# A fused attention, soft mixture and feed-forward kernel: w_in kept by halves, four more weight slots, and the first unit of the feed-forward stage cut in two

## The chip, the cores and the metric

The kernel runs on one NeuronCore of one Trainium2 chip. Its engines are TensorE (PE, with its weight loads shown as PEld), VectorE (DVE), ScalarE (ACT), GpSimd (POOL) and SyncE (SP, which here only issues DMAs). The metric is the device time of one execution in microseconds (us). The time before is a median of 460.08 us over 3 runs, from 459.59 to 461.58 us. The execution that the profiler took lasted 463.19 us, of which the recorded span is 461.4 us.

## The reference

Three layers, one after the other. The inputs are float32, but for w_in and w_out, which come as float64; the output is float32.

```python
# 1. causal attention, 4 batches x 8 heads, 576 tokens, 64 wide
scores = q @ k.T / 8
bias   = -(cumsum(max(s, 0))[:, None] - cumsum(max(s, 0))[None, :])
attn   = softmax(where(causal, -1e9, scores + min(bias, 0)))
x      = attn @ v                        # gathered to [2304, 512]
# 2. soft mixture: 32 slots, 8 experts with 4 slots each
logits = x @ phi
slot_input = softmax(logits, tokens).T @ x          # [32, 512]
slot_out[e] = max(slot_input[e] @ w1[e], 0) @ w2[e] # w1 512x1024, w2 1024x512
x = softmax(logits, slots) @ slot_out
# 3. feed-forward
h = x @ w_in                             # 512 -> 2048
g = where(h >= 1, h, where(h <= -1, 0, (h + 1)**2 / 4))
out = g @ w_out                          # 2048 -> 512
```

The kernel never forms the second x. Since x = c @ slot_out with c of 32 columns, h = c @ (slot_out @ w_in), and the product M = slot_out @ w_in is only 32 x 2048. M is kept as a stack of 96 rows (`mst`: its rounded part twice, its rest once), against 96 rows of c (`cstack`), so that one matmul in the fast fp32r type gives h to float32's precision.

## The kernel before

**Attention.** 16 pairs of heads run one after the other. Each has four groups of score matmuls (line 291), row maxima on DVE (line 305), exponentials on ACT (line 350), transposes and products with v on PE. A table of numbers (`PLAN`, 12 units of plan time to a pair) says when each step's instructions are written, and `GATE` does so for the gating of one batch, which falls into the pairs 5, 9 and 13 and the one after each.

**Conversion of w_in.** It arrives as float64 words, 2048 columns by 512, in four quarters `fb` of 512 columns (a quarter is 2 MB raw and 1 MB as float32). During attention a generator (`convert_wi`) brings it chunk by chunk: a 256 KB DMA to `st`, one POOL operation (line 626), then two DVE operations (lines 627 and 629); each call of the generator issues one of the two. The pairs 1 to 13 call it, up to five times each. All four quarters stay in `wif`, 32 KB per partition. `finish_wi` later runs four DVE operations on each of 16 tiles.

**Weights of the experts.** w1 and w2 of 8 experts are 64 tiles of 512 KB, loaded by SP (line 140) into slots. 22 slots exist from the start (16 of kind "post", 6 of kind "pre"), filled during attention; 13 are cut out of attention's right-hand memory when that is free, 3 more after it; from there on a load waits for a slot that PE has done with. SP issues in program order and waits in place, so a load that waits holds all that is behind it.

**Experts.** For each expert `layer1` (line 736, 16 matmuls), a transpose, `layer2` (line 752, 32 matmuls). The last one gives `soT`, the transposed slot outputs.

**Feed-forward.** 96 units (j, c), j one of 6 blocks of 384 tokens, c one of 16 blocks of 128 hidden columns. A unit is: `h_part` (one matmul at line 879, relu and square on ACT at 881 and 882), `g_part` (max on DVE at 889, rounding to gh on ACT at 891), `l_part` (the rest gl on DVE at 897), `o_part` (nine matmuls at 907 to 909). The output matmuls of a unit are written two units after its `h_part`. The first 32 units alternate between j = 0 and 1, so that c advances every second unit, and through the first 30 of them w_out is converted (`convert_wo`: ACT at 154 and 786, DVE at 156, 158 and 788), one tile of 512 columns per two units. Its raw tiles come into "pre" slots.

M is computed ahead of the loop, in parts, by `m_part`: 16 matmuls of 128 columns for the first 128 columns of each quarter, all four quarters at once in four groups of 32 rows, then 16 of 384 columns. `split_m` writes the first quarter's stack on ACT and DVE, `stack_m` moves the other three quarters' rows into place by nine DMAs. The order is

```python
m_part(0, M_A, range(4))
split_m(0, M_A)
...
h_part(*seq[0])
h_part(*seq[1])
m_part(M_A, 512, range(1, 4))
g_part(*seq[0])
g_part(*seq[1])
```

Of the kernel before, what the change touches and what calls it, by code (L numbers as in the profile page):

```python
# [8 lines left out]
F32 = mybir.dt.float32  # L9
# [22 lines left out]
N_HOME = 16  # L32
N_LEFT = 6
N_RIGHT = 6
N_TMP = (7, 3)
# [15 lines left out]
WI_0 = (0,)  # L51
WARM_T = (9, 4, 2, 3, 4)
PRE_FROM, PRE_STEP = (5, 2.4)
# [3 lines left out]
BLK = 384  # L57

# [13 lines left out]
def attention_softmoe_ffn_kernel(  # L72
# [31 lines left out]
    wif = wip.tile([128, 4, 4, 512], F32, name="wif")  # L104

    w_src = {"w1": w1, "w2": w2, "wo": w_out.bitcast(I32)}
    w_tiles, w_wo, wo_used = {}, {}, []
# [58 lines left out]
    with att:  # L166
# [436 lines left out]
        for n in range(N_HOME + N_LEFT):  # L603
            at(3 * int(PRE_FROM + PRE_STEP * n) + 0.76, lambda: next(pre, None))

        def convert_wi():

            n_all = 2048 * 4 // CHUNK
            sts = {}

            def get(n):
                if n < n_all:
                    fb, k = divmod(n, 2048 // CHUNK)
                    sts[n] = stage.tile([128, 2 * CHUNK], I32, tag="st", name="st")
                    nc.sync.dma_start(out=sts[n], in_=w_in.bitcast(I32)[fb, :, 2 * CHUNK * k:2 * CHUNK * (k + 1)])

# [3 lines left out]
            for n in range(n_all):  # L620
                fb, k = divmod(n, 2048 // CHUNK)
                st = sts.pop(n)
                d = wif[:, fb].rearrange("p c f -> p (c f)")[:, CHUNK * k:CHUNK * (k + 1)]
# [3 lines left out]
                V.tensor_scalar(lo, lo, 1, 0x70000000, op0=ALU.logical_shift_right, op1=ALU.bitwise_and)  # L627
                yield
                V.tensor_tensor(out=d.bitcast(I32), in0=d.bitcast(I32), in1=lo, op=ALU.bitwise_or)
                get(n + 2)  # L630
                yield

        def finish_wi():

            for n in range(16):
# [11 lines left out]
        for pi in range(NP):  # L647
# [15 lines left out]
            for k in range(5) if pi else WI_0:  # L663
                step(f"W{k}", next, cw, None)
# [178 lines left out]
    M_A = 128  # L843
    mp = [ps_e.tile([128, 512], F32, tag="e", name="mp") for _ in range(2)]

    def m_part(a, b, cs):
        for c in cs:
            for fb in range(4):
                T.matmul(out=mp[a > 0][32 * fb:32 * fb + 32, a:b], lhsT=soT[:, c], rhs=wif[:, fb, c, a:b],
                         start=(c == 0), stop=(c == 3))  # L850

    m_hi = fin[0].tile([128, 512], F32R, tag="m_hi", name="m_hi", bufs=1)
    m_lo = fin[0].tile([128, 512], F32R, tag="m_lo", name="m_lo", bufs=1)
    ps_w = []

    def split_m(a, b):
# [158 lines left out]
```

## Time and profile before

| | |
|---|---|
| median of 3 runs | 460.08 us |
| profiled execution | 463.19 us (span 461.4 us) |
| PE busy | 443.8 us, 96% of the span |
| ACT busy | 339.0 us, 73% |
| DVE busy | 326.7 us, 71% |
| POOL busy | 45.3 us, 10% |
| DMA | 71.02 MB, mean 154 GB/s over the span |

The shares are averages over three stages with different limits. Attention lasts to about 193 us, the experts from there to 237 us, the feed-forward stage to the end. A busy PE in this table includes matmuls that stand in its pipeline and wait, so that 96% does not say that nothing else sets the time; the chain of waits and the stretches do.

### The profile page before, as it was taken

What the parts mean: (1) busy time and instruction counts of PE and PEld (TensorE: products, weight loads), DVE (VectorE), ACT (ScalarE), POOL (GpSimd) and SP (SyncE); (2) the same over time, 40 slices, a digit from 0 to 9 for tenths busy, and PEclk for the clock granted to TensorE, in tenths of its full rate; (3) what the DMA queues carried; (4) which work ended last, traced back from release to release, by engine and by line L of the source; (5) the groups of instructions that cost most, each with busy time, mean ns of one, the idle gap of its engine ahead of it and who ended that gap; (6) DMA issues with size and microseconds to landing.
All of it is one profiled execution on the core that took longest, in us unless ns stands there. A gap on an engine that the chain in (4) does not pass through costs nothing.

```text
span 461.4 us, 11656 instructions
## 1 busy us (share of the span) xinstructions
PE 443.8 (96%) x4306; PEld 336.8 (73%) x4306; DVE 326.7 (71%) x966; ACT 339.0 (73%) x914; POOL 45.3 (10%) x168
## 2 busy tenths in 40 slices
PE   7999999999999998898889999999999999999996
PEld 2676766776777676566546888888888888888885
DVE  6687899899988863699838888866555555455543
ACT  6998998998999894122248999977677767777673
POOL 2222212422222111000000000000000000000000
PEclk9799999999999998799999999999999999999999
DMA  3888879977897258699985900003001001001001
GB/s 86 228 219 217 255 218 294 265 225 192 221 279 237 67 170 287 216 390 407 409 294 196 362 2 1 0 2 136 1 0 68 1 1 70 1 0 56 14 1 68
DMA packets 28554, 71.02 MB, mean 154 GB/s; under 512 B 4018, under 2 KB 5490, under 8 KB 28498
## 3 DMA queue, kind: packets, MB, share of 16 engines
q1 hardware_dynamic: 28342, 70.14, 47.7%
q8 instruction: 34, 0.56, 0.5%
q14 instruction: 22, 0.18, 0.2%
q10 hardware_dynamic: 156, 0.14, 0.1%
HBM read 64.83 MB, written 4.83 MB: 151 GB/s over the span
## 4 chain that ended last, share of the span: by engine, by line
PE 83%; DVE 6%; DMA 5%; ACT 4%; issue 2%; POOL 0%; ACTq 0%; POOLq 0%; DVEq 0%; SPq 0%
PE o L909 14%; PE o L907 14%; PE o L908 14%; PE s L291 9%; PE s L399 7%; PE s L360 5%; DMA wt<-in_w_dram 4%; PE hp L879 4%; PE s L434 3%; PE p L736 2%; PE s L299 2%; PE s L391 2%; PE p L752 2%; ACT P L350 1%; DVE s L305 1%
## 5 line engine op out<-in xcount | busy, mean ns | idle before, releaser
L907 PE MATMUL o<-wt,gh 128*128 128x512 f32 x288 | 112.6, 391 | 0.6 <-ACT gh L891 0.6
L909 PE MATMUL o<-wt,gl 128*128 128x512 f32 x288 | 112.3, 390 | 0.2 <-DVE gl L897 0.2
L908 PE MATMUL o<-wt,gh 128*128 128x512 f32 x288 | 112.1, 389 | 0.0
L350 ACT ACTIVATE P<-s,nm 128x256 f32<-128x256 f32 (+4 forms) x160 | 85.0, 551 | 9.1 <-DVE nm L305 6.8
L897 DVE TENSOR_TENSOR gl<-g,gh 128x384 fp32r<-128x384 f32 x96 | 53.5, 557 | 42.1 <-ACT gh L891 42.0
L305 DVE CUSTOM_DVE_ANT_0 s<-s,tri 128x256 f32<-128x256 f32 (+4 forms) x160 | 74.0, 506 | 12.6 <-PE s L291 6.2
L891 ACT CAST gh<-g 128x384 fp32r<-128x384 f32 x96 | 49.3, 513 | 45.1 <-DVE g L889 42.6
L889 DVE SCALAR_TENSOR_TENSOR g<-w,hp 128x384 f32<-128x384 f32 x96 | 53.1, 553 | 37.2 <-ACT w L882 37.2
L907 PEld LDWEIGHTS o<-wt,gh 128*128 128x128 f32 x288 | 54.3, 188 | 12.8 <-ACT gh L891 1.1
L909 PEld LDWEIGHTS o<-wt,gl 128*128 128x128 f32 x288 | 54.0, 188 | 12.5 <-DVE gl L897 1.3
L908 PEld LDWEIGHTS o<-wt,gh 128*128 128x128 f32 x288 | 54.4, 189 | 7.5
L291 PE MATMUL s<-x 64*128 64x512 f32 (+3 forms) x256 | 57.1, 471 | 0.0
L881 ACT ACTIVATE w<-hp,half 128x384 f32<-128x384 f32 x96 | 55.4, 577 | 0.8 <-PE hp L879 0.8
L882 ACT ACTIVATE w<-w 128x384 f32<-128x384 f32 x96 | 50.4, 525 | 3.0
L383 ACT COPY pts<-s 128x512 f32<-128x512 f32 (+3 forms) x128 | 47.8, 463 | 1.5 <-PE s L360 0.5
L360 PEld LDWEIGHTS s<-ident,P 64*128 64x128 f32 x800 | 38.6, 142 | 10.9 <-ACT P L350 4.8
L360 PE MATMUL s<-ident,P 64*128 64x64 f32 x800 | 44.2, 229 | 2.3 <-ACT P L350 2.2
L399 PE MATMUL s<-pts,v 128*64 128x512 f32 (+3 forms) x256 | 38.9, 446 | 0.0
L350 ACT ACTIVATION_READ_ACCUMULATOR P<-s,nm 128x1 f32 x160 | 36.8, 230 | 0.0
L879 PE MATMUL hp<-cstack,mst 96*128 96x384 f32 x96 | 32.6, 343 | 0.3 <-DVE mst L859 0.3
L291 PEld LDWEIGHTS s<-x 64*128 64x128 f32 x256 | 29.3, 196 | 4.2 <-DMA x<-in_qkT_dram 1.5
L399 PEld LDWEIGHTS s<-pts,v 128*64 128x64 f32 x256 | 18.5, 141 | 17.5 <-issue 15.3
(149 smaller groups left out, 567.2 us busy)
## 6 DMA issues: line engine op xcount, KB each, us to landing
wt<-in_w_dram SPq DMA_DIRECT2D x64, 512.0 KB
x<-in_qkT_dram SPq DMA_DIRECT2D x32, 288.0 KB
st<-in_w_in_dram SPq DMA_DIRECT2D x32, 256.0 KB
wt<-in_w_out_dram SPq DMA_DIRECT2D x16, 512.0 KB
out_dram<-ob SPq DMA_DIRECT2D x17, 256.0 KB
v<-in_v_main_dram SPq DMA_DIRECT2D x16, 256.0 KB
ext<-exts SPq DMA_DIRECT2D x60, 3.4 KB
v<-in_v_tail_dram SPq DMA_DIRECT2D x16, 32.0 KB
```

The source lines that it names most:

```text
L291: T.matmul(out=o[h][:, off:off + n], lhsT=y[r, 0, c:c + 128], rhs=y[r, 1, 0:n], start=(k == 0), stop=(k == 1))
L305: V.tensor_tensor_reduce(out=sc, in0=sc, in1=mask[:, mask.shape[1] - n:], scale=-1.0 / SCALE, scalar=init, op0=ALU.add, op1=ALU.min, accum ...
L350: A.activation(out=out_, in_=in_, func=AF.Exp, bias=nm, scale=-1.0, accum_out=sm[:, k:k + 1])
L360: T.transpose(out=o[f][:, c:c + 64], in_=P[r], identity=ident[r, r])
L399: T.matmul(out=o[r, 128 * j:512], lhsT=vt[:, j, r], rhs=pts_t[pi][:, h, 512 * j:384 * j + 512], start=(j == 0), stop=(j == 3))
L879: T.matmul(out=hp, lhsT=mst[0:96, 128 * c:128 * c + 128], rhs=cstack[0:96, BLK * j:BLK * j + BLK], start=True, stop=True)
L881: A.activation(out=w, in_=hp, func=AF.Relu, bias=half, scale=0.5)
L889: V.scalar_tensor_tensor(out=g, in0=w, scalar=1.0, in1=hp, op0=ALU.min, op1=ALU.max)
L897: V.tensor_tensor(out=gl, in0=g, in1=gh.bitcast(F32), op=ALU.subtract)
L907: T.matmul(out=o_t[j][t], lhsT=gh[:, r], rhs=wh[c], start=(c == 0), stop=False)
L908: T.matmul(out=o_t[j][t], lhsT=gh[:, r], rhs=wl[c], start=False, stop=False)
L909: T.matmul(out=o_t[j][t], lhsT=gl[:, r], rhs=wh[c], start=False, stop=(c == 15))
```

## The change

The quarters of w_in get three fates. Quarters 0 and 1 stay in `wif` as before (`WI_KEEP`). Quarter 2 is converted in attention too, wholly, with three DVE operations per chunk, and each chunk is stored to a DRAM tile (`w_in_f`), to be read back after the experts' weights (`WI_AWAY`). Quarter 3 is loaded raw after the experts' weights and converted inside the feed-forward loop, in four pieces at the units 5, 8, 11 and 14 (`WI_LATE`, `LATE_AT`). `wif` so needs 16 KB per partition less, and four more weight slots take that place (`N_LEFT` 6 to 10). The generator is called in the pairs of `W_PAIRS` alone, five times each, and twice in pair 0; 26 weight loads are spread over attention and not 22.

The first 128 columns of M are computed three times into 96 rows, so that the stack is one cast over 96 rows and one subtraction. The first unit's activation is done in a part of 128 and one of 256 tokens. M's quarter 2 and 3 are computed inside the loop, in the units 10 and 18 (`M_AT`), by 16 matmuls each, and stacked by twelve DMAs per quarter.

```diff
-N_LEFT = 6
+N_LEFT = 10
+WI_KEEP = 2
+WI_AWAY = (2,)
+WI_LATE = (3,)
+W_PAIRS = (1, 2, 3, 4, 6, 7, 8, 10, 11, 12, 14)
...
-WI_0 = (0,)
+WI_0 = (0, 3)
-PRE_FROM, PRE_STEP = (5, 2.4)
+PRE_AT = [3 * int(5 + 2.4 * _n) + 0.76 for _n in range(22)] + [171.76, 177.76, 183.76, 186.76]
+M_AT = {10: 2, 18: 3}
+LATE_AT = 5
...
                 G.tensor_scalar(d, hi.bitcast(F32), 2.0 ** -112, 1.0, op0=ALU.mult, op1=ALU.mult)
-                V.tensor_scalar(lo, lo, 1, 0x70000000, op0=ALU.logical_shift_right, op1=ALU.bitwise_and)
+                if away:
+                    V.tensor_scalar(lo, lo, 29, None, op0=ALU.logical_shift_right)
+                    yield
+                    V.scalar_tensor_tensor(out=di, in0=di, scalar=3, in1=lo, op0=ALU.logical_shift_left, op1=ALU.bitwise_or)
+                    yield
+                    V.scalar_tensor_tensor(out=di, in0=hi, scalar=-0x80000000, in1=di, op0=ALU.bitwise_and, op1=ALU.bitwise_or)
+                else:
...
+                get(n + 2)
+                put()
+                if away:
+                    spill.append((fb, k, d))
                 yield
...
-            for n in range(16):
+            for n in range(4 * WI_KEEP):
...
+    def load_wi():
+
+        for fb in WI_LATE:
+            for c in range(4):
+                raw, slot = slot_tile(I32)
+                nc.sync.dma_start(out=raw, in_=w_in.bitcast(I32)[fb, :, 1024 * c:1024 * c + 1024])
...
+                late.append((convert(raw, out_, out_), slot))
+        for fb in WI_AWAY:
+            for n in range(2):
+                t = slot_tile()[0]
+                nc.sync.dma_start(out=t, in_=w_in_f[fb][:, 1024 * n:1024 * n + 1024])
...
+    def h_part(j, c, fb=None):
+        hm = ps_h.tile([128, 512], F32, tag="h", name="hp")
+        hp = hm[:, 0:BLK]
         T.matmul(out=hp, lhsT=mst[0:96, 128 * c:128 * c + 128], rhs=cstack[0:96, BLK * j:BLK * j + BLK], start=True, stop=True)
+        if fb is not None:
+            m_part(hm[:, BLK:512], back(fb))
...
+    def first_m():
+
+        m = ps_o.tile([96, 128], F32, tag="o1", name="m0")
+        for c in range(4):
+            for r in range(3):
+                T.matmul(out=m[32 * r:32 * r + 32, :], lhsT=soT[:, c], rhs=wif[:, 0, c, 0:128], start=(c == 0), stop=(c == 3))
+        A.copy(out=mst[0:96, 0:128], in_=m)
+        V.tensor_tensor(out=mst[64:96, 0:128], in0=m[64:96], in1=mst[64:96, 0:128].bitcast(F32), op=ALU.subtract)
...
+    load_wi()
     one_c = gens[WO_EARLY]
     next(one_c)
-    m_part(0, M_A, range(4))
-    split_m(0, M_A)
     next(one_c)
+    first_m()
+    m_part(mp[0], kept(0))
+    first_unit()
+    h_part(*seq[1])
+    for fb in range(1, WI_KEEP):
+        m_part(mp[fb], kept(fb))
     next(one_c)
-    m_part(M_A, 512, range(1))
-    h_part(*seq[0])
-    h_part(*seq[1])
-    m_part(M_A, 512, range(1, 4))
-    g_part(*seq[0])
     g_part(*seq[1])
...
+    for g in range(1, 4):
+        split_m(mp[0], g)
+    for fb in range(1, WI_KEEP):
+        stack_m(fb, mp[fb])
...
+        for n, k in late_at.get(i, []):
+            for _ in range(k):
+                next(late[n][0])
```

SP's queue from the end of attention to the feed-forward stage, before (wt is an expert's or w_out's tile, gate a wait for the last expert weight, mst M's stack):

```order
L140 DMA wt<-in_w_dram 128x1024 x38
L140 DMA wt<-in_w_out_dram 128x1024
L140 DMA wt<-in_w_dram 128x1024 x4
L140 DMA wt<-in_w_out_dram 128x1024
L133 DMA gate<-wt 1x1
L140 DMA wt<-in_w_out_dram 128x1024 x6
L867 DMA mst<-m_hi 32x512 x2
L867 DMA mst<-m_lo 32x512
```

and after the change (wi is w_in's late and read-back tiles, w_in_f_147 the DRAM tile):

```order
L148 DMA wt<-in_w_dram 128x1024 x36
L148 DMA wt<-in_w_out_dram 128x1024
L148 DMA wt<-in_w_dram 128x1024 x4
L148 DMA wt<-in_w_out_dram 128x1024
L141 DMA gate<-wt 1x1
L148 DMA wt<-in_w_out_dram 128x1024 x5
L908 DMA wi<-in_w_in_dram 128x1024 x4
L917 DMA wi<-w_in_f_147 128x1024 x2
L148 DMA wt<-in_w_out_dram 128x1024
L893 DMA mst<-m_hi 32x128 x2
L893 DMA mst<-m_lo 32x128
```

Of the loads that stand in one run behind attention's last input, 38 become 36, of which the first two belong to the 26; six loads of w_in stand between w_out's.

ACT's order at the start of the feed-forward stage, before (w, gh, hp are a unit's tiles, cv is w_out's conversion, mst and m_hi M's stack):

```order
L761 COPY soT<-p_4782 128x4x4
L154 ACTIVATE cv<-wt 128x512
L858 CAST mst<-mp 32x128 x2
L881 ACTIVATE w<-hp,half 128x384
L882 ACTIVATE w<-w 128x384
L881 ACTIVATE w<-hp,half 128x384
L882 ACTIVATE w<-w 128x384
L891 CAST gh<-g 128x384 x2
L858 CAST mst<-mp 32x384 x2
L863 CAST m_hi<-mp 128x128
L863 CAST m_hi<-mp 128x384
L154 ACTIVATE cv<-wt 128x512
L881 ACTIVATE w<-hp,half 128x384
```

and after, up to the same place:

```order
L1001 CAST mst<-m_4763 96x128
L1013 ACTIVATE w<-hp,half 128x128
L1016 ACTIVATE w<-w 128x128
L1013 ACTIVATE w<-hp,half 128x256
L1020 CAST gh<-g 128x128
L1016 ACTIVATE w<-w 128x256
L1020 CAST gh<-g 128x256
L939 ACTIVATE w<-hp,half 128x384
L940 ACTIVATE w<-w 128x384
L951 CAST gh<-g 128x384
L883 CAST mst<-mp 32x128 x6
L889 CAST m_hi<-mp 128x128
L162 ACTIVATE cv<-wt 128x512
L939 ACTIVATE w<-hp,half 128x384
```

The two first units were interleaved and follow one another now; the first one is in two parts, and the casts for M's stack are six of 128 columns in place of two of 384.

PE in unit 10 after the change (the h product, then M's quarter 2 into the same tile, then the output products of unit 8):

```order
L969 MATMUL o_4913<-wt,gl 128x512
L935 MATMUL hp<-cstack,mst 128x384
L876 MATMUL hp<-wi,soT 32x128 x16
L967 MATMUL o_4842<-wt,gh 128x512
L968 MATMUL o_4842<-wt,gh 128x512
L969 MATMUL o_4842<-wt,gl 128x512
```

Before, line 879's product stood there alone; the 16 matmuls of 128 columns are new in this place, and 16 more stand in unit 18.

## Rows read from the trace of the kernel before

**Rows 1.** The page's first line and its chain that ended last, by engine

```profile
span 461.4 us, 11656 instructions
...
PE 83%; DVE 6%; DMA 5%; ACT 4%; issue 2%; POOL 0%; ACTq 0%; POOLq 0%; DVEq 0%; SPq 0%
```

**Rows 2.** Stretches: start:end and length, busy (instructions) per engine, clock, DMA share, GB/s

```profile
87.88:97.47 9.59, 9.59 (x146) 7.22 (x146) 8.45 (x35) 9.22 (x34) 3.12 (x11) 1.00 0.83 230
97.47:120.23 22.76, 22.67 (x331) 15.63 (x330) 20.84 (x91) 19.62 (x70) 4.92 (x21) 1.00 0.79 213
198.00:234.00 36.00, 32.17 (x724) 22.75 (x717) 31.41 (x58) 9.05 (x29) 0.00 (x0) 1.00 1.02 403
237.27:253.00 15.73, 14.55 (x108) 8.83 (x107) 11.16 (x23) 12.79 (x28) 0.61 (x1) 1.00 0.70 235
253.00:298.00 45.00, 45.00 (x205) 37.86 (x204) 37.29 (x73) 42.49 (x83) 0.00 (x0) 1.00 0.26 95
307.00:350.00 43.00, 43.00 (x196) 36.22 (x195) 23.76 (x43) 30.22 (x60) 0.00 (x0) 1.00 0.10 37
```

**Rows 3.** Chain in order of time, expert stage: start us, length us, engine, tile, line

```profile
199.24 1.75 PE p L752 x64
...
211.39 0.65 PE p L752 x22
...
215.30 10.26 DMA wt<-in_w_dram
...
235.82 0.64 PE p L752 x16
...
237.67 1.08 PE mp L849 x32
```

**Rows 4.** Timeline of ACT at the feed-forward's start: start us, length us, instruction

```profile
237.27 0.17 ACT L761 COPY soT<-p 128x16 f32<-128x16 f32 x1 [0.34 <-PE p L760]
...
240.15 0.58 ACT L881 ACTIVATE w<-hp,half 128x384 f32<-128x384 f32 x1 [0.85 <-PE hp L879]
...
246.19 0.58 ACT L881 ACTIVATE w<-hp,half 128x384 f32<-128x384 f32 x1
```

**Rows 5.** Timeline of PE, the first output product

```profile
242.76 0.50 PE L907 MATMUL o<-wt,gh 128*128 128x512 f32 x1 [0.41 <-ACT gh L891]
```

**Rows 6.** Timeline of ACT, two units of the feed-forward stage

```profile
290.80 0.66 ACT L154 ACTIVATE cv<-wt 128x512 f32<-128x512 f32 x1
...
291.51 0.51 ACT L891 CAST gh<-g 128x384 fp32r<-128x384 f32 x1
...
295.14 0.66 ACT L154 ACTIVATE cv<-wt 128x512 f32<-128x512 f32 x1
```

**Rows 7.** Timeline of PE, the hidden products of the same two units

```profile
291.32 0.34 PE L879 MATMUL hp<-cstack,mst 96*128 96x384 f32 x1
...
295.76 0.34 PE L879 MATMUL hp<-cstack,mst 96*128 96x384 f32 x1
```

**Rows 8.** Instructions grouped by form: busy us, mean ns | idle before

```profile
L629 DVE TENSOR_TENSOR wif<-wif,st 128x256 int32<-128x256 int32 x32 | 14.0, 438 | 0.1
...
L158 DVE SCALAR_TENSOR_TENSOR cv<-cv,wt 128x512 int32<-128x512 int32 x16 | 11.0, 687 | 0.7 <-DMA wt<-in_w_dram 0.5
...
L154 ACT ACTIVATE cv<-wt 128x512 f32<-128x512 f32 x16 | 10.5, 658 | 0.0
...
L627 DVE TENSOR_SCALAR st<-st 128x256 int32<-128x256 int32 x32 | 9.4, 292 | 0.3
...
L156 DVE TENSOR_SCALAR wt<-wt 128x512 int32<-128x512 int32 x16 | 6.8, 422 | 1.8 <-DMA wt<-in_w_out_dram 1.8
...
L739 ACT ACTIVATE hs<-p 128x256 f32<-128x256 f32 x8 | 3.1, 385 | 15.6 <-PE p L736 15.6
...
L757 ACT COPY os<-p 128x128 f32<-128x128 f32 x8 | 2.1, 266 | 17.0 <-PE p L752 17.0
```

**Rows 9.** Who SyncE's queue waited for: us in total, times, longest

```profile
SPq L218 <- DMA wt<-in_w_dram: 6.9, 5, 2.5
```

More of the change, by code (lines that the diff above doesn't have):

```diff
@@ L662, in attention_softmoe_ffn_kernel @@
                     step(n, f, pi)
-            for k in range(5) if pi else WI_0:
+            for k in (range(5) if pi in W_PAIRS else ()) if pi else WI_0:
                 step(f"W{k}", next, cw, None)
@@ L840, in attention_softmoe_ffn_kernel, with m_part @@
             conv.setdefault(max(1, NWIN * n + CONV_AT + f), []).append(n)
[L843 to L849, printed above, removed]
+    mp = [ps_e.tile([128, 128], F32, tag="e", name="mp") for _ in range(WI_KEEP)]
+    ps_w = []
+    def m_part(out, w):
+        for c in range(4):
+            for g in range(4):
+                T.matmul(out=out[32 * g:32 * g + 32, :], lhsT=soT[:, c], rhs=w(c)[:, 128 * g:128 * g + 128],
@@ L861, in stack_m @@
[L861 to L870 removed]
+            A.copy(out=mst[32 * r:32 * r + 32, c], in_=m[q])
@@ new lines, in split_m, with stack_m @@
+        V.tensor_tensor(out=mst[64:96, c], in0=m[q], in1=mst[0:32, c].bitcast(F32), op=ALU.subtract)
+    def stack_m(fb, m):
+        m_hi, m_lo = (fin[0].tile([128, 128], F32R, tag=n, name=n, bufs=2) for n in ("m_hi", "m_lo"))
+        A.copy(out=m_hi, in_=m)
+        V.tensor_tensor(out=m_lo, in0=m, in1=m_hi.bitcast(F32), op=ALU.subtract)
+        for g in range(4):
+            for r in range(3):
+                nc.sync.dma_start(out=mst[32 * r:32 * r + 32, 512 * fb + 128 * g:512 * fb + 128 * g + 128].bitcast(F32),
+                                  in_=(m_hi if r < 2 else m_lo)[32 * g:32 * g + 32].bitcast(F32))
@@ L873, in attention_softmoe_ffn_kernel, with kept, back @@
+    late = []
+    def kept(fb):
+        return lambda c: wif[:, fb, c]
+    def back(fb):
+        return lambda c: w_wi[fb, c]
     NB = NTOK // BLK
@@ L883, in h_part @@
         g_t[j, c] = hp, w
+        if fb is not None:
+            return lambda: stack_m(fb, hm[:, BLK:512])
     def g_part(j, c):
@@ L951, in attention_softmoe_ffn_kernel @@
     o_next()
-    split_m(M_A, 512)
-    stack_m()
+    for g in range(1, 4):
+        split_m(mp[0], g)
+    for fb in range(1, WI_KEEP):
+        stack_m(fb, mp[fb])
+    ps_e_ctx.close()
+    ps_w.append(ctx.enter_context(tc.tile_pool(name="ps_w", bufs=2, space=PSUM)))
+    late_at = {}
+    for n in range(len(late)):
+        for f in range(2):
+            late_at.setdefault(LATE_AT + 3 * n + 2 * f, []).append((n, 2 - f))
     for i in range(1, len(seq) + 1):
+        stack = None
         if 2 < i:
@@ L963, in attention_softmoe_ffn_kernel @@
             o_next()
+        if stack:
+            stack()
     while done[1] < len(seq):
```

89 lines of the change are left out of this document (57 added, 32 removed).

## The prediction, made before the changed kernel had run

> **What bounds the kernel now.** I read the page's first line and its chain first: 461.4 us, 83% of the chain on PE [rows 1]. That share mixes three stages, so I next cut the span into stretches [rows 2], where the reader is to see which engine is full in which stage. In a plain pair of heads PE is busy all of 9.59 us and DVE 8.45. Over a gate's two pairs PE is busy 22.67 of 22.76 us. In the experts' stage the DMA share is 1.02 at 403 GB/s from 198 to 234 us while PE has 3.8 us idle: the loads set the time. From 253 to 298 us PE is busy throughout, but ACT is too, 42.49 of 45 us, with DVE at 37.29; after the conversion of w_out ACT falls to 30.22 of 43. The chain in order of time then says what ends the experts' stage: from 215.30 us on it lies on the weight DMA, until the last product starts at 235.82 [rows 3]. Last I read the timelines around the feed-forward's start and in its middle [rows 4 to 7], for who waits for whom there.
>
> **The experts' loads: -5.2 us.** Four tiles of 512 KB less are left when attention ends. At 403 GB/s [rows 2] one takes 524,288 / 403,000 = 1.30 us, four 5.2. For this to be the gain three things must hold. The four must land beside attention: SP's order has them behind the last pairs' inputs, and the stretch of a gate's pairs has a DMA share of 0.79 [rows 2], so there is room. The DMA must stay full after them: each later load takes a slot freed earlier, and with 42 slots in place of 38 by then none waits longer. And PE must not become the limit: layer 2 of two experts three apart starts at 199.24 and 211.39 us [rows 3], 4.05 us per expert, so that the eighth would start at 211.39 + 4 x 4.05 = 227.6 and end 1.75 later at 229.3, against 235.82 + 0.64 = 236.5 now. PE's slack is 7.1 us, more than 5.2. So the end of the stage moves to about 231.3; the bounds are 0 and the slack of 7.1, and I take 5.2. The trace's rate weighs against a page here. The Trainium skill, page HBM Reference, sections Specifications (TRN2) and Access, gives a core some 358 GB/s as its share and about 425 when it streams alone; by the first, four loads would be an estimated 5.9 us, by the second 4.9. The trace's 403 lies between, and the sum keeps 5.2.
>
> **finish_wi: 0.** Eight of 16 tiles go, four DVE operations each. DVE was busy 31.41 of the 36 us there [rows 2], but the loads hide that, and they still do when it is half.
>
> **Attention: -0.8 us.** The conversion's DVE operations leave the gate's pairs 5, 9 and 13. There were five in such a pair, alternately 0.292 and 0.438 us [rows 8], some 1.8 us, so a gate may gain 0 to 1.8. PE idles visibly 0.09 us in these two pairs [rows 2]; their 3.58 us over two plain ones (22.76 - 2 x 9.59) are then mostly PE's own gate products. I take 0.25 per gate, near that row. The third DVE operation per chunk of quarter 2 costs no call of its own, since each call still issues one operation, in pairs where PE is the full engine. The eight stores of quarter 2 stand in SP's queue before the inputs of later pairs; how they delay those the trace doesn't show. SP waited for a weight DMA before a pair's small rows five times, 6.9 us in all [rows 9], and it came to no visible wait of PE. I take nothing, and keep 0 to +6 for the range.
>
> **The feed-forward's start: +0.5 us.** Counted from soT at 237.27 [rows 4], the first relu starts 2.9 us later, the first output product 5.5 [rows 5], the third unit's relu 8.9. M's first part takes 1.08 us [rows 3] and is followed now by another of its kind before the first h product, whose stack is one cast less: no change at the first relu. In two parts, an ACT operation costs 0.266 + 0.385 = 0.65 us by the rows for 128 and 256 columns [rows 8], against 0.51 for a whole cast [rows 6]. The first output product needs the first part alone: relu, square, max, cast at about 0.27 each with the larger relu in between: about 4.2 us after soT, 1.3 sooner. But ACT runs in order: three split operations cost 0.3 us more together, the two units are no longer interleaved so that ACT waits about 0.5 us for DVE twice where it hardly did, and of M's casts six small replace two and one. That is +1.3 if all of it counts, and -1.3 if the earlier product does. PE waits for ACT here, so I stay on ACT's side, but not at its end, since DVE has gaps to catch up in (11.16 of 15.73 us [rows 2]): the third unit's relu 0.5 us later. The Trainium skill, page Perfetto Trace Analysis, section Optimizing Scalar/DVE Operations, says that breaking up instructions may let work finish sooner where these engines are not saturated, and that larger ones pay where they are. ACT is busy 12.79 of 15.73 us at this start [rows 2] and full right behind it; by the first half of that rule the term would be -1.3, by the second above 0.
>
> **The late quarters: +3.5 us.** In the loop PE's period is (295.76 - 291.32) / 2 = 2.22 us per unit [rows 7], ACT's (295.14 - 290.80) / 2 = 2.17 [rows 6]: ACT gains 0.10 us on PE per two units, and it comes out of the start late. Four pieces of quarter 3 add one ACT operation each, worth the 0.71 us from one start to the next [rows 6], and the unit 10 one cast of 0.27 [rows 8]: 3.1 us between the units 5 and 14, of which it gains 0.5 back. So PE is 2.6 us late by unit 14. The product for quarter 2 in unit 10, half of layer 2's 1.75 us for 32 such matmuls [rows 3], 0.88 us, lies inside this. The one in unit 18 finds ACT no longer behind by more than its buffers, and adds its 0.9. Together 3.5. Cheapest case: ACT's lag is hidden and only 2 x 0.88 = 1.8 us of PE remain. Dearest: DVE's four pairs of operations (0.422 + 0.687 each [rows 8], 4.4 us) wait in turn with ACT's instead of beside them, 3.1 + 4.4 + 0.9 = 8.4. DVE had 7.7 us idle in the 45 [rows 2], so I stay near the row of ACT. M's stack by twelve small DMAs per quarter has some six units to arrive: 0; and after unit 30 ACT has 12.8 us idle in 43 [rows 2], so nothing is left over.
>
> **Sum.** -5.2 - 0.8 + 0.5 + 3.5 = -2.0 us on the profiled execution of 463.19, which gives 461.2. That execution lies 3.1 us above the median of 460.08; the difference carries over, and the prediction is 458.1 us.
>
> **Rivals.**
> A, the late quarters cost PE's products alone, and the start gains 0.5: -5.2 - 0.8 - 0.5 + 1.8 = -4.7, 455.4 us. For it: two units of buffering between h and its output product, and ACT's 2.5 us idle in 45. Against: ACT leaves the start late and gains only 0.10 us per two units.
> B, ACT and DVE wait for each other: M's stacks, the conversion of w_out and that of quarter 3 stand in one order, and each square, max, cast and rest crosses twice between the two. Half of DVE's 4.4 us on top is +2.2, which gives 460.3, no change. For it: ACT at 94% of the stretch; against: DVE at 83%.
> C, slower: SP's queue in attention. If each of the eight stores holds the inputs behind it by the mean 1.4 us of [rows 9] and five of them come late to PE, attention loses 7 us and the sum is +5.0, 465.1. It decides once a pair's rows land after PE has reached them; today PE shows no such wait in the stretches.
> D, the loads are not what ends the stage any more: if PE, with less time to wait, runs at 4.9 us per expert and not 4.05, its slack of 7.1 shrinks to 3.7 and 1.5 us of the gain goes: 459.6.
>
> **How the numbers follow.** About 0.5% (2.3 us) is what a measurement can tell from no change: 457.8 and 462.4 are the bounds. The forecast has 0.42, its own range 456.5 to 459.8, of which 0.40 lies below 457.8; A has 0.25, B 0.15, C 0.10, D 0.08. Faster: 0.42 x 0.40 + 0.25 + a little of B = 0.44. Slower: C and the upper end of B, 0.14. The rest, 0.42, is no change. The range takes in A with 1.5 us of more gain in the gates, to 454.0, and B to the middle of its dear side, to 461.8.
>
> **What would show it.** The DMA should stay at 400 GB/s to a last landing near 230.6 us, and the first output product come 4.2 us after soT. Between the units 5 and 18 the h products' distance should rise from 2.22 to about 2.5, with waits for ACT. The 32 new matmuls should stand there for 0.9 us each 16. Attention should end some 0.8 us sooner. I am wrong if soT doesn't come about 6 us earlier, if the loop keeps 2.22 through the late pieces, or if PE waits for a pair's inputs in attention.

## The result and the profile after

The changed kernel takes 462.08 us (median of 19 executions, 459.19 to 466.44), the kernel before 459.59 beside it: ratio 1.0055 [1.0035, 1.0075], 2.5 us slower. The forecast was 458.1 with a range from 454.0 to 461.8, so it was wrong in sign.

The profiled execution after takes 461.27 us. First the page's span and chain by engine, which answer to [rows 1]:

```profile
span 459.5 us, 11848 instructions
...
PE 89%; ACT 5%; DVE 3%; issue 1%; DMA 1%; SPq 0%; POOL 0%; ACTq 0%; POOLq 0%
```

The DMA has left the chain (5% before, 1% now). The stretches that answer to [rows 2], in the same columns (start:end and length, busy and instructions of PE, PEld, DVE, ACT, POOL, granted clock, DMA share, GB/s): a plain pair, a gate's two pairs, the experts, the first 15.73 us behind soT, the next 45, and a late stretch.

```profile
87.31:96.90 9.59, 9.59 (x144) 7.22 (x144) 8.66 (x37) 9.22 (x33) 3.20 (x11) 1.00 0.78 227
96.90:119.23 22.33, 22.33 (x328) 15.45 (x328) 19.57 (x85) 19.84 (x70) 3.71 (x17) 1.00 0.73 198
190.00:226.00 36.00, 33.58 (x751) 23.91 (x748) 17.28 (x32) 9.73 (x31) 0.00 (x0) 1.00 1.00 389
228.34:244.07 15.73, 12.02 (x120) 8.66 (x119) 8.57 (x20) 10.86 (x28) 0.61 (x1) 0.89 1.00 373
244.07:289.07 45.00, 44.67 (x252) 36.08 (x251) 38.61 (x77) 41.03 (x82) 0.00 (x0) 1.00 0.35 115
298.00:341.00 43.00, 43.00 (x195) 36.20 (x194) 25.32 (x46) 31.18 (x62) 0.00 (x0) 1.00 0.10 38
```

The gate's pairs are 0.43 us shorter (22.76 to 22.33). In the experts' stage DVE has half its work left, and PE is at 33.58 of 36 us. Behind soT PE, ACT and DVE all do less than before in the same time (12.02 against 14.55, 10.86 against 12.79, 8.57 against 11.16 us): they wait for each other. The chain of the experts' stage, in the columns of [rows 3]:

```profile
197.08 1.75 PE p L778 x64
...
201.17 1.75 PE p L778 x64
...
205.26 0.65 PE p L778 x22
205.91 0.86 issue
206.77 1.50 PE p L778 x42
...
212.11 0.75 issue
...
224.43 0.57 PE p L778 x15
...
225.43 0.48 PE idle L756 x3
225.91 0.57 PE p L778 x16
```

It runs on PE from product to product. Two experts without a stop are 4.09 us apart (197.08 to 201.17). Twice PE stops inside an expert's second layer, for 0.86 and 0.75 us ("issue": the profile shows nothing that it waits for), and these two experts take 5.35 and 5.24 us. Before, two pieces of 10 us in this chain lay on a weight DMA; now there is none. SyncE's gate, which waits for the last expert weight, and PE's first product with that weight, before and after:

```profile
235.79 0.67 SPq L133 DMA_DIRECT2D gate<-wt  x1
235.82 0.64 PE L752 MATMUL p<-wt,hT 128*32 128x128 f32 x16
```

```profile
226.07 0.68 SPq L141 DMA_DIRECT2D gate<-wt  x1
226.89 0.65 PE L778 MATMUL p<-wt,hT 128*32 128x128 f32 x16
```

Before, PE started as soon as the weight was there; now the weight is there 0.8 us earlier. The three groups of idle transposes between the quarters of this last matrix, 0.48 us each, filled waits before and stand in the chain themselves now. From the first expert product to the last copy of soT the stage takes 40.0 us, before 44.1. Then the start, to be read against [rows 4, 5], on ACT and PE:

```profile
228.34 0.17 ACT L787 COPY soT<-p 128x16 f32<-128x16 f32 x1 [0.34 <-PE p L786]
...
231.03 0.37 ACT L1013 ACTIVATE w<-hp,half 128x128 f32<-128x128 f32 x1 [0.96 <-PE hp L1023]
...
232.81 0.50 PE L967 MATMUL o<-wt,gh 128*128 128x512 f32 x1 [0.64 <-ACT gh L1020]
...
237.68 0.53 ACT L883 CAST mst<-mp 32x128 fp32r<-32x128 f32 x2 [0.99 <-DVE mst L884]
237.79 0.59 PE L935 MATMUL hp<-cstack,mst 96*128 96x384 f32 x2 [2.11 <-DVE mst L884]
...
239.85 0.57 ACT L939 ACTIVATE w<-hp,half 128x384 f32<-128x384 f32 x1
```

The first output product comes 4.5 us after soT instead of 5.5, as forecast (4.2). But PE then waits 2.11 us for M's second 128 columns, and the third unit's relu comes 11.5 us after soT instead of 8.9. And unit 10, with quarter 2's products inside, against [rows 7]:

```profile
256.62 0.34 PE L935 MATMUL hp<-cstack,mst 96*128 96x384 f32 x1
256.89 1.08 PE L876 MATMUL hp<-wi,soT 128*32 128x128 f32 x32
...
260.07 0.34 PE L935 MATMUL hp<-cstack,mst 96*128 96x384 f32 x1
```

The distance is 3.45 us where a plain unit has 2.22: 1.23 us for the 16 products (two instructions each in the trace).

### The profile page after: what moved, and what is told of

Read it like the earlier page. It is cut to its first block, busy times and chain, and to the rows that moved or that the text cites. A ratio compares the mean times of both kernels' runs of the same rounds, so it can differ in the third digit from the quotient of the medians.

```text
span 459.5 us, 11848 instructions
## 1 busy us (share of the span) xinstructions
PE 440.2 (96%) x4394; PEld 337.3 (73%) x4394; DVE 312.5 (68%) x939; ACT 341.0 (74%) x925; POOL 42.0 (9%) x160
## 4 chain that ended last, share of the span: by engine, by line
PE 89%; ACT 5%; DVE 3%; issue 1%; DMA 1%; SPq 0%; POOL 0%; ACTq 0%; POOLq 0%
PE o L969 13%; PE o L967 13%; PE o L968 13%; PE s L299 9%; PE s L407 8%; PE s L368 6%; PE s L442 4%; PE p L778 3%; PE p L762 3%; PE hp L935 3%; PE s L307 3%; PE s L399 3%; PE s L533 1%; DMA x<-in_qkT_dram 1%; ACT P L358 1%
## 5 line engine op out<-in xcount | busy, mean ns | idle before, releaser
L967 PEld LDWEIGHTS o<-wt,gh 128*128 128x128 f32 x288 | 54.6, 189 | 14.1 <-ACT gh L1020 1.6
L299 PE MATMUL s<-x 64*128 64x512 f32 (+3 forms) x256 | 54.9, 462 | 0.2 <-DMA x<-in_qkT_dram 0.2
L368 PE MATMUL s<-ident,P 64*128 64x64 f32 x800 | 42.5, 227 | 2.6 <-ACT P L358 2.4
L358 ACT ACTIVATION_READ_ACCUMULATOR P<-s,nm 128x1 f32 x160 | 37.9, 237 | 0.0
L407 PE MATMUL s<-pts,v 128*64 128x512 f32 (+3 forms) x256 | 37.3, 433 | 0.0
L299 PEld LDWEIGHTS s<-x 64*128 64x128 f32 x256 | 28.3, 191 | 3.4 <-DMA x<-in_qkT_dram 1.7
L407 PEld LDWEIGHTS s<-pts,v 128*64 128x64 f32 x256 | 17.2, 137 | 17.0 <-issue 14.6
```

What stands on the lines that cost most here:

```text
L299: T.matmul(out=o[h][:, off:off + n], lhsT=y[r, 0, c:c + 128], rhs=y[r, 1, 0:n], start=(k == 0), stop=(k == 1))
L358: A.activation(out=out_, in_=in_, func=AF.Exp, bias=nm, scale=-1.0, accum_out=sm[:, k:k + 1])
L368: T.transpose(out=o[f][:, c:c + 64], in_=P[r], identity=ident[r, r])
L407: T.matmul(out=o[r, 128 * j:512], lhsT=vt[:, j, r], rhs=pts_t[pi][:, h, 512 * j:384 * j + 512], start=(j == 0), stop=(j == 3))
L967: T.matmul(out=o_t[j][t], lhsT=gh[:, r], rhs=wh[c], start=(c == 0), stop=False)
```

## The experiments

All are compared with the kernel before on the same chip. The two numbers on the right, from each run's timeline, localize the time in us: from the last copy of soT to unit 9's product of M and c (the start), and from there to unit 95's (86 plain distances of 2.22 are 190.9; what is above is late work and stalls).

| kernel | median us | ratio [interval] | soT to unit 9 | unit 9 to 95 |
|---|---|---|---|---|
| before, first profile | 459.59 | | 23.0 | 190.9 |
| changed | 462.08 | 1.0055 [1.0035, 1.0075] | 25.6 | 194.6 |
| e1_before_again | 459.85 | 1.0001 [0.9976, 1.0026] | 23.1 | 190.9 |
| e2_split_early | 462.58 | 1.0054 [1.0030, 1.0079] | 24.9 | 194.7 |
| e3_no_late_work | 459.44 | 0.9988 [0.9966, 1.0010] | 25.6 | 190.9 |
| e4_slots_held | 467.03 | 1.0149 [1.0111, 1.0187] | 25.6 | 194.6 |
| e5_start_as_before | 462.56 | 1.0061 [1.0036, 1.0087] | 23.9 | 196.2 |
| e6_casts_first | 461.63 | 1.0035 [1.0012, 1.0057] | 24.7 | 194.7 |
| e7_steps_in_gate_pairs | 464.81 | 1.0096 [1.0064, 1.0129] | 25.6 | 194.6 |
| e8_conversions_only | 460.60 | 1.0014 [0.9993, 1.0036] | 26.8 | 192.1 |
| e9_old_start_casts_first | 463.15 | 1.0097 [1.0070, 1.0124] | 24.2 | 196.1 |
| e10_m2_in_start | 462.88 | 1.0066 [1.0037, 1.0095] | 23.1 | 196.1 |
| e11_no_late_no_start | 456.89 | 0.9932 [0.9908, 0.9957] | 23.0 | 190.9 |
| e12_late_on_gpsimd | 464.27 | 1.0101 [1.0064, 1.0138] | 26.3 | 197.2 |
| e13_fifth_ob | 461.82 | 1.0019 [0.9992, 1.0047] | 23.0 | 195.5 |
| e14_filled_idle | 463.79 | 1.0069 [1.0045, 1.0093] | 25.6 | 194.7 |
| e15_both | 459.00 | 0.9987 [0.9962, 1.0013] | 23.1 | 194.6 |
| e16_quarter3_in_attention | 469.64 | 1.0198 [1.0171, 1.0225] | 23.2 | 193.3 |
| e17_tail_warm_both | 457.51 | 0.9928 [0.9899, 0.9957] | 23.0 | 194.7 |
| e18_tail_warm_changed | 460.93 | 1.0014 [0.9992, 1.0036] | 25.6 | 194.7 |

**e1_before_again**: the kernel before, once more.

> The kernel before, unchanged, run beside itself: ratio 1.000. What it is for: its profiled execution lasted 463.19 us against a median of 459.6, so a second profile with the granted clock of each run. If the 3.6 us were clock alone, the new profile should have its slot outputs (soT) some 3 us earlier than 237.27 us and the same 224 us from there to the end; if the profiled execution was typical, soT lies at 237 us again.

It ran 459.85. Its profile has the experts' stage at 43.8 us and the start at 23.1, but its first expert product at 188.1 us, where the profile behind my prediction has 193.1. Dates of single profiles differ by 5 us ahead of the experts; the distances behind them differ by 0.3 us at most.

**e2_split_early**: the second 128 columns' split ahead of the first unit.

```diff
     m_part(mp[0], kept(0))
+    split_m(mp[0], 1)
     first_unit()
...
-    for g in range(1, 4):
+    for g in range(2, 4):
         split_m(mp[0], g)
```

> The changed kernel with the stack of M's second 128 columns written before the first unit's activation, not after the second unit's. Theory S (the start is where the loss is: the third unit's h product waits 2.11 us for that stack, and PE's clock is then halved for 3.4 us): the wait goes, 1.5 to 2.5 us less than the changed kernel, 459.6 to 460.6. Rival L (the loop behind it is bound by ACT, so that an earlier h product only waits later): no change, 462.

PE's wait of 2.1 us goes, unit 9 comes only 0.8 us sooner, and the time stays. PE's wait is a symptom: ACT, whose casts still wait 0.99 us for DVE in this trace, sets the start.

**e3_no_late_work**: no late conversions, no products and stacks of quarters 2 and 3.

> The changed kernel without the late quarters' work: no conversion of quarter 3, no products for quarters 2 and 3 in the units 10 and 18, no stacks of them (these columns of M are set to zero instead); all loads stay. By the h products' distances in the trace the late work costs 3.7 us: 458.4. If only PE's 32 matmuls count: 2 x 1.08 = 2.2 us less, 459.9. Whatever is left over the kernel before is then the start's.

The late work costs 1.0055 - 0.9988 = 0.0067, 3.1 us, by the ratios and 3.7 by the table's last column.

**e4_slots_held**: the four added slots stay empty until w_in's late quarters take them.

```diff
-PRE_AT = [3 * int(5 + 2.4 * _n) + 0.76 for _n in range(22)] + [171.76, 177.76, 183.76, 186.76]
+PRE_AT = [3 * int(5 + 2.4 * _n) + 0.76 for _n in range(22)]
...
-    w_free = list(wpre)
+    w_free = list(wpre[:-4])
...
+    w_free += wpre[-4:]
     load_wi()
```

> The changed kernel with the four added slots kept empty until the feed-forward stage, and 22 weight loads in attention as before. If four slots are worth four loads at 403 GB/s: +5.2 us on the changed kernel, 467.3. If the experts' stage were limited by PE by now, less than +2.

The slots are worth 1.0149 - 1.0055 = 0.0094, 4.3 us by the ratios, with an uncertainty of 2.0; in the traces the experts' stage takes 44.8 us and not 40.0. Neither tells them from the 5.2 of the forecast.

**e5_start_as_before, e6_casts_first, e9_old_start_casts_first**: the start undone in two halves and whole. e5:

```diff
+    m_part(mp[0], kept(0))
+    split_m(mp[0], 0)
     next(one_c)
-    first_m()
-    m_part(mp[0], kept(0))
-    first_unit()
+    next(one_c)
+    h_part(*seq[0])
     h_part(*seq[1])
...
-    next(one_c)
+    g_part(*seq[0])
     g_part(*seq[1])
     next(one_c)
+    l_part(*seq[0])
     l_part(*seq[1])
```

> The changed kernel with the feed-forward's first two units in before's order: M's quarter 0 by one chain of 16 products, its first 128 columns split, both units whole and interleaved (relu and square of each, then both g, then both low halves). The second to fourth 128 columns are still split in three steps behind them. Theory S (the start costs 2.6 us because the parts of one unit wait for each other on ACT and DVE with no second unit between them): unit 2's relu starts 9 to 10 us behind the last copy of soT, not 11.5, and the kernel takes 460.1 us (459.3 to 460.9), about 2 us less than the change's 462.1. Rival T (the loss is in attention, from the quarters' steps that share pairs with the gates' neighbours and the stores to DRAM): no change, 462.1 (461.5 to 462.7). Rival W (the granted clock falls to half more often in the changed kernel, wherever PE has a short idle): gain only if the half-clock stretch of 3.4 us at 240 us goes, at most 1.7 us.

e6 issues the six casts of `split_m` for g = 1 to 3 and then the three subtractions:

> The changed kernel with the order of the three splits behind the first unit changed: all six ACT casts of M's columns 128 to 512 first, then the three DVE subtractions. In the changed kernel's trace each pair of casts waits for the subtraction before it (0.99 and 0.36 us). Theory S: ACT runs through the six casts, unit 2's relu comes 1.2 us sooner (10.3 us behind soT), and the kernel takes 460.9 us (460.3 to 461.7). Rivals T and W: no change, 462.1.

e9 is both:

> The changed kernel with both edits on the start: the first two units in before's order (as in e5_start_as_before) and all ACT casts of the three splits ahead of their subtractions (as in e6_casts_first). In their traces the one brought the loop 1.65 us and the other 1.0 us forward against the changed kernel. Theory S: together they undo the start's whole excess, unit 9's product of M and c starts 23.0 us behind the last copy of soT (before 22.9 to 23.1, changed kernel 25.7), and the kernel takes 459.5 us (458.8 to 460.3). Rival U (the executions of e5_start_as_before were no shorter, 462.6 us, so what is won at the start is lost again elsewhere, as in the 1.5 us that DVE waited there for a store of the output): 461.5 to 462.5 us.

The traces do what theory S says: the first two units in before's order win 1.7 us, casts first 0.9, both together 2.6 to 2.7 where nothing disturbs it (e11, e13, e15 and e17 have the same start: 23.0 to 23.1). e6 keeps its 0.9 us in the time (ratio 1.0035). But e5 and e9 are no shorter at all, as rival U had it. Their traces show why. In e9's profile the granted clock falls to 0.5 (1.2 GHz, the lower of TensorE's two levels) in PE's wait of 1.47 us for the first cast and stays there for 6.8 us, so that an output product that takes 0.40 us takes 0.63, and unit 9 comes 1.2 us later than in the others:

```profile
235.67 0.79 PE L969 MATMUL o<-wt,gh 128*128 128x512 f32 x1 [1.47 <-ACT gh L953]
236.26 0.63 PE L970 MATMUL o<-wt,gh 128*128 128x512 f32 x1
```

And behind units 30 and 31, where six output tiles go to DRAM through four buffers, DVE waits for a buffer (e5, 1.80 us; e9 has 1.78):

```profile
316.08 0.69 DVE L155 COPY ob<-o 128x512 f32<-128x512 f32 x1 [1.80 <-DMA out_dram<-ob]
```

PE loses 1.5 us there. In the trace's packet records a 16 KB packet of the queue that the page lists as `q8 instruction` starts 1.2 us after the stores' first packet. In six of the 20 profiles (e5, e9, e10, e12, e13, e16) such a packet starts 0.2 to 1.2 us after that first packet, and the copies into the buffers, DVE's and in e10 and e12 one of ACT's, wait 1.1 to 3.4 us; in the other 14 it is at least 4.8 us away, the six stores are through in 5.0 us, and no copy waits. In the kernel before, from 300 us on, these packets lie 246 to 263 instructions of PE apart, so their place seems to move with the number of instructions ahead of them. (The 324 to 326 us in e13's expectation count from the trace's first record, 11 us ahead of the span's start.) The Trainium skill, page Runtime: NRT & Kernel Launch, section Instruction fetch mechanics, says that engines fetch their instructions in 16 KiB blocks and that crossing a block is mostly hidden. The size agrees; here it wasn't hidden. The stops in the experts' stage may be of the same kind: counted through PE's instructions, the two in the changed kernel lie 256 apart, and all 20 profiles, the kernel before's too, have the second at that count to within one, 0.75 to 1.02 us long. No run tests it.

By the sums of the table's two columns e5 and e9 are as long as the changed kernel, to 0.2 us. e9's time is longer than that, by 1.9 us in the ratios with an uncertainty of 1.5; its trace doesn't show where.

**e7_steps_in_gate_pairs**:

```diff
-W_PAIRS = (1, 2, 3, 4, 6, 7, 8, 10, 11, 12, 14)
+W_PAIRS = tuple(range(1, 12))
```

> The changed kernel with the quarters' conversion steps in pairs 1 to 11, five in each, as many in all, so that the pairs with a gate (5 and 9) have them again. My prediction priced this term at +0.25 us for each such pair: 462.6 us (462.1 to 463.1). Rival T (attention is slower because the steps now run to pair 14 and hold up the tail): 461 us or less.

The interval of a gate is counted between the starts of its two pairs' products for `phi` (line 442 of the changed kernel). In e7's trace those of two gates grow from 11.91 to 12.11 and from 11.96 to 12.42 us: +0.66, near the priced 0.5. The time grew by 1.9 by the ratios, from six executions; what the rest is I don't know. The intervals show that keeping the steps out of the gates gains.

**e8_conversions_only**: the late conversions stay, the products and stacks go.

> The changed kernel with the late conversions of quarter 3 kept, but M's products and stacks for quarters 2 and 3 in units 10 and 18 left out (those columns of M are zero). Theory P (the late work costs what PE spends on 16 products each time, 1.23 us twice, since the loop is PE's there): the kernel takes 459.6 us (459.0 to 460.3), near the run without any late work. Rival A (the conversions' operations on ACT and DVE cost it, as my prediction had it, 2.6 of 3.5 us): 461.6 us (461.0 to 462.3).

460.6 lies between the two ranges. By the ratios the conversions cost 1.2 us (1.0014 - 0.9988) and the products 1.9 (1.0055 - 1.0014), each with an uncertainty near 1.5. The trace doesn't settle it: its start met a stretch of 6.8 us at half clock (granted 0.5; unit 9 at 26.8), in which ACT may have caught up.

**e10_m2_in_start**, on top of e9, and **e12_late_on_gpsimd**, on top of e10. e10:

```diff
-M_AT = {10: 2, 18: 3}
+M_AT = {18: 3}
...
+    m_part(m_all[:, 128:256], back(2))
```

> e9_old_start_casts_first with quarter 2 read back ahead of w_out's loads and M's product of it moved from unit 10 to the start, behind the product of quarter 1, where PE has 1.4 us of idle before the first output product. Its stack is made with quarter 1's by one cast and one subtraction of 256 columns. Theory S (PE's 1.23 us in unit 10 are saved, ACT's 0.1 to 0.3 us more at the start are paid): 458.4 us (457.6 to 459.3), below the kernel before. Rival: quarter 2's tile lands too late or the w_out loads behind it do, and ACT or PE waits: 459.5 us or more.

> e10_m2_in_start with quarter 3's late conversions taken off ACT: the scaling by 2^-112 on GpSimd, and three DVE operations a chunk in place of two. Theory S with ACT as what the conversions cost (0.43 + 0.22 + 0.52 us of longer distances): 457.6 us (456.8 to 458.5). Rival V (DVE is as full as ACT there, or GpSimd's operation slows DVE's): no gain or a loss against e10_m2_in_start.

Neither gained. In e10 the 1.23 us leave unit 10, but the extra distances at the conversions grow from 1.2 us (0.43, 0.22, 0.52 in the changed kernel) to 2.6 (0.47, 0.60, 0.54, 0.98). ACT is busy 20.35 of 22.20 us there, and as I read it PE's product had covered half of its lag. The stall at the stores adds 1.3. This profile is e10's shortest execution, 459.79 us; what makes the others up to 465.55 is not shown. e12's profile shows a candidate, the rival that e10's expectation names: PE waits in the start for quarter 2's read-back tile.

```profile
237.07 0.64 PE L894 MATMUL mp<-wi,soT 128*32 128x128 f32 x16 [2.50 <-DMA wi<-w_in_f]
```

That is most of the 3.2 us by which e12's unit 9 comes later than e10's. Behind it GpSimd's operation slows DVE's, which take 0.55 us alone:

```profile
250.57 1.09 POOL L936 TENSOR_SCALAR wi<-wi 128x512 f32<-128x512 f32 x1 [0.57 <-DMA wi<-in_w_in_dram]
...
251.07 1.00 DVE L979 TENSOR_TENSOR gl<-g,gh 128x384 fp32r<-128x384 f32 x1
```

The Trainium skill, page SBUF — State Buffer, section Who interferes with whom, says that a DVE operation with two inputs from SBUF contends with a GpSimd one that reads it; the 1.00 us agrees. From unit 9 on e12 is 1.1 us longer than e10, 0.5 of it at the stores.

**e11_no_late_no_start**: e9 without late work.

> e9_old_start_casts_first without late work: no conversions of quarter 3, no products and stacks of quarters 2 and 3 (those columns of M are zero); their loads stay. What is left of the change is the weights' four slots, the shorter finish and the quarters' steps in attention. Theory S (the change's time is the sum of weights -4.2, start +2.65, late work +3.7 and attention near -0.5 us, with nothing else): 455.6 us (454.8 to 456.5). Rival U: 458 to 459.5 us, as e3_no_late_work had it.

Its feed-forward stage is before's to 0.1 us. What is left of the change, slots and attention, is worth 3.1 us [2.0, 4.2] by the ratio.

**e13_fifth_ob, e14_filled_idle, e15_both**: a fifth output buffer on e9; PE's idle time in the changed kernel's start filled; and e13 with PE's idle time filled.

```diff
-                ob = ew.tile([128, 512], F32, tag="ob", name="ob", bufs=4)
+                ob = ew.tile([128, 512], F32, tag="ob", name="ob", bufs=5)
```

> e9_old_start_casts_first with five buffers in place of four for the output rows on their way to DRAM. Theory F (in the kernels with the old start a 16 KB fetch of instructions falls at 324 to 326 us into the six stores behind units 30 and 31, the second store lands late, DVE's sixth copy waits 1.8 us for its buffer and PE loses 1.5 us; with five buffers the sixth copy needs only the first store): the distances between h products stay at 2.22 us behind unit 30, and the kernel takes 461.6 us (460.9 to 462.4), against 463.15 of e9_old_start_casts_first. Rival: PE loses the time to something else there and the stall stays: 463 us.

> The changed kernel with 18 transposes of the identity into unused columns of unit 1's PSUM tile, behind unit 0's output products, where PE waits 2.1 us for M's second 128 columns. Theory W (that idle time lets the granted clock fall to half for 3.4 us just behind it, which delays the loop): no half-clock stretch at 240 us, unit 9's h product up to 1 us sooner, 461.3 us (460.6 to 462.0). Theory S (ACT sets the start, the clock only takes what PE had to spare): no half-clock stretch and no change, 462.1 us (461.5 to 462.8).

> e13_fifth_ob with 11 transposes in PE's 1.5 us of idle time ahead of the first output product, where the execution of e9_old_start_casts_first fell to the half clock for 6.8 us. With the start undone, the stall at the stores gone and the clock kept up, theory S with F and W gives 1.1 us less than e13_fifth_ob at most: 460.0 us (459.2 to 461.2). Rival: the transposes delay the output products behind them: 462 us or more.

e13's stall shrank from 1.5 to 0.8 us; the fifth buffer covers only part of it. e14 shows the changed kernel's start at the full clock (the changed kernel itself had 0.89 in this stretch):

```profile
230.70:246.43 15.73, 13.78 (x142) 9.83 (x140) 8.53 (x20) 10.81 (x28) 0.61 (x1) 1.00 0.92 341
```

and unit 9 where it was, 25.6: the half clock cost nothing at this start, ACT sets it, as theory S has it. (The median of 463.8 lies above both ranges; six of its 12 executions have the low mean clock that e17 and e18 are about.) In e15 the start is before's, no clock falls there, and the added instructions moved the 16 KB packet to 4.8 us ahead of the stores: no stall. It is 3.1 us shorter than the changed kernel by the ratios (1.0055 - 0.9987), near e9's forecast at last.

**e16_quarter3_in_attention**, on top of e13: quarter 3 converted, stored and read back as quarter 2 is, with conversion steps in every pair.

```diff
-WI_AWAY = (2,)
-WI_LATE = (3,)
-W_PAIRS = (1, 2, 3, 4, 6, 7, 8, 10, 11, 12, 14)
+WI_AWAY = (2, 3)
+WI_LATE = ()
+W_PAIRS = tuple(range(1, 16))
```

> e13_fifth_ob with no late conversions: quarter 3 is converted in attention as quarter 2 is, stored to DRAM and read back, with conversion steps in all pairs, the gates' too; quarter 2's products of M stand in the start, quarter 3's in unit 16. Theory S: of the late work only one product's 1.23 us is left, the gates get back 0.9 us: 458.6 us (457.6 to 460), below the kernel before. Rival T (e7_steps_in_gate_pairs lost 1.9 us by the ratios for two gates): 460 us or more.

The late work fell to 2.4 us, 1.2 of it the stall at the stores, and yet the kernel lost 9. Who SyncE's queue waited for (total, times, longest), and the chain of its experts' stage:

```profile
SPq L149 <- DVE wif L668: 14.1, 1, 14.1
```

```profile
209.41 10.11 DMA wt<-in_w_dram
...
219.59 10.16 DMA wt<-in_w_dram
...
229.81 10.14 DMA wt<-in_w_dram
```

The conversions now last to the end of attention, a weight load whose slot is cut from their space waits 14.1 us for the last of them, and the loads behind it in the queue set the stage. The changed kernel ends its steps in pair 14.

**e17_tail_warm_both, e18_tail_warm_changed**: six transposes more in attention's last gate, on e15 and on the changed kernel.

```diff
-WARM_T = (9, 4, 2, 3, 4)
+WARM_T = (9, 7, 5, 3, 4)
```

> e15_both with six more transposes of the identity in attention's last gate: WARM_T (9, 7, 5, 3, 4) for (9, 4, 2, 3, 4), three each in PE's waits of 0.52 and 0.43 us there. In the profiled executions of the changed family a half-clock stretch of 3.4 or 10.2 us begins in this tail, and the executions with a mean granted clock below 0.9835 are 2 to 4 us longer than those above 0.9905, where the kernel before has few such executions and no difference. Theory C (the tail's half clock, met once the weights arrive sooner, takes part of what the slots win): hardly an execution is left below 0.9835 and the median falls to 458.3 us (457.5 to 459.2). Rival: the transposes delay the chain by what they fill, or the clock falls elsewhere: 459 to 460.5 us.

> The changed kernel with the same six transposes in attention's last gate and nothing else. Theory C: the executions below 0.9835 go and the median comes to those of the changed kernel at a high clock, 460.8 us (460.0 to 461.7). Rival: no change, 462.1 us (461.6 to 463).

Both came true. Three stretches from the last gate's products for `phi` to the first expert product, the changed kernel's, e14's and e17's:

```profile
176.40:188.32 11.92, 10.09 (x94) 6.90 (x95) 7.65 (x30) 3.69 (x15) 0.58 (x2) 0.86 0.73 257
```

```profile
176.53:189.91 13.38, 11.54 (x95) 7.92 (x96) 7.67 (x30) 3.68 (x15) 0.58 (x2) 0.73 0.67 239
```

```profile
177.12:187.77 10.65, 9.34 (x100) 7.07 (x101) 7.66 (x30) 3.68 (x15) 0.57 (x2) 1.00 0.83 300
```

The same work, in e17 with six transposes more, takes 11.92, 13.38 and 10.65 us at mean granted clocks of 0.86, 0.73 and 1.00 (1.00 is 2.4 GHz, half of it 1.2). e17 beats both kernels, 0.9928 [0.9899, 0.9957] of before.

## Why the prediction was wrong

Three runs split the change, since each leaves out one part more: e11 (slots and attention), e3 (and the start), the changed kernel (and the late work). Each measured term has an uncertainty of 1.1 to 1.5 us.

| term | forecast us | measured by ratios us |
|---|---|---|
| experts' loads and attention | -6.0 | -3.1 (e11) |
| feed-forward's start | +0.5 | +2.6 (e3 against e11) |
| late quarters | +3.5 | +3.1 (changed against e3) |
| sum | -2.0 | +2.5 |

**The feed-forward's start failed.** The step "+1.3 if all of it counts" was its upper bound, and 2.6 was measured (traces: 2.7). I had seen all its parts, and sized them too small: from soT to the third unit's relu ACT's idle time grew from 2.6 to 4.6 us and its work from 6.3 to 6.9. One unit in two parts is a chain ACT to DVE to ACT with no second unit beside it; and M's three splits behind it took turns, each pair of casts waiting for the subtraction before (0.99 and 0.36 us; e6 won 0.9 by order alone). I had counted the splits as six operations, not as a chain that crosses twice between engines. And "DVE has gaps to catch up in" is the wrong way round: gaps in both engines are what such a chain looks like.

**The experts' loads and attention failed in size, in two places.** One is the step "PE's slack is 7.1 us, more than 5.2". The prediction's sum gives PE 37.0 us from the first expert product to the last copy of soT (193.1 to 229.3, and 0.8 behind it); in the changed kernel's chain, with no weight DMA in it, PE takes 40.0. Above all the sum left out the two stops, 1.6 us together, and the three groups of idle transposes, 1.4. [rows 3] had a sign of it: the fourth expert's line reads 0.65 us x22 and not 1.75 x64, because PE stops there. So the slack was 4.1 us, and the change uses all of it: counted from the first product, the last weight is there 4.9 us sooner, soT 4.1. Over 16 profiles of the changed kernel and its variants (without e4 and e16) the stage takes 39.4 to 41.5 us, with a median of 40.3, against 44.1 and 43.8 before: 3.6 us gained, not 5.2. Rival D, at 0.08, had this effect, though not its rate: it set 4.9 us per expert, and the measured mean is 4.3.

The other is attention's end, for which the prediction has no term. The gates gave 0.9 together (e1's intervals 11.98, 12.36, 12.37 against 11.91, 11.96, 11.96), where I had 0.8. Yet e1's first expert product comes at the changed kernel's date, 188.1 and 188.3. The stretch from the last gate's products for `phi` to that product takes 10.64 us in e1 and 11.92 in the changed kernel, with 3.4 us of it at half clock; of the profiles of the changed kernel and its variants up to e16, 12 of 16 have 11.9 to 13.4 us there. By the times, of 18 executions of the changed kernel the 7 at a mean clock below 0.9835 took 464.3 us, the 4 above 0.9905 took 460.5 (means); the kernel before took 459.7 to 460.0 at any clock, and 3 of 124 executions were below 0.9835. e18 and e17 took 1.9 and 2.7 us away by keeping PE busy there. Why the change is hit more often stays open. The kernel before isn't spared: its first profile, at a mean clock of 0.98, has half clock at attention's end too and 11.95 us there, and its first product comes 5.0 and its soT 5.35 us later than e1's, so its slack swallowed none of that. I haven't run these transposes in the kernel before, so how much of their gain needs the change is open as well.

**The late quarters were right in sum, not in their parts.** I had 2.6 us of ACT with the first product inside, and 0.9 of the second. A product takes PE 1.23 us (priced 0.88). The conversions add 1.2 us beside two products and 2.6 beside one (e10), so the first product does lie in ACT's lag, as the forecast had it: 2.6 for the conversions and 1.2 for the second product make 3.8, against 3.7 in the changed kernel's trace. The product's wrong price enters once, because the first one is hidden. Rival A, PE's products alone, would not have let e10's distances grow.

**Of the signs I named**, the h distances rose and attention's gates shortened as said. The first output product came 4.5 us after soT, as said, and won nothing. The last weight had landed by 226.1, not 230.6, and soT is 9 us earlier than in [rows 4] and 3.6 earlier than in e1: a date compared between two single profiles proved nothing. Rival C did not show: plain pairs stay at 9.59 us, so the stores delayed no input of a pair there. Rival B's price did not show in the late quarters, but ACT and DVE waiting for each other is what lengthened the start.

## What to carry to other kernels

Price a cut of one unit into parts as a chain: count each crossing between two engines, and ask which second unit fills the waits; without one, the earlier first product bought nothing here. Before booking a gain from earlier loads, add up the other engine's whole chain, with its stops and the filler instructions that only stand in waits so far, and take its length from more than one execution. And when an edit that surely helps in the trace doesn't help the time, look for stalls elsewhere that moved with the instruction count.

## What was unexpected

A 16 KB packet of the instruction queue beside six stores went with 1.1 to 3.4 us of waiting for a buffer, six times in six, and cost PE 0.8 to 1.7 us. With six transposes of 0.1 us in two waits of 0.5 us the granted clock stayed at 1.00 through attention's end in both profiles, 1.3 to 2.7 us less there, while 3.4 us of half clock at the feed-forward's start cost nothing (e14), where ACT sets the pace: what the clock costs depends on whether PE is the bound. PE stopped twice, 256 of its instructions apart, in the stage where the DMA is full, for a reason that the profile doesn't name. And a load that waits in SyncE's queue for a slot (14.1 us in e16) delays everything behind it.
